# Attention with two feed-forward layers on one core: weight loads, score stacks and one preparation moved at the beginning

## The chip, the cores and the metric

The kernel runs on one core of a Trainium2 chip. The metric is the device time of one execution in microseconds (us). The core has five instruction streams: TensorE (PE, with its weight loads as PEld), VectorE (DVE), ScalarE (ACT), GpSimd (POOL) and SyncE (SP), which here only issues transfers. Each stream runs its instructions in the order in which they stand in the program, and an instruction that waits holds up all that stand behind it.

## The reference

```python
scores = scale * q @ k.T                       # 4 batches, 8 heads, 576 tokens, head size 64
cum    = cumsum(log(clip(f, 1e-4, 1)))         # a decay per token
scores = where(causal, -1e9, scores + cum[i] - cum[j])
attn   = softmax(scores) @ v                   # -> x: 2304 tokens x 512
h = x @ w_in;   x = (h * tanh(softplus(h))) @ w_out      # d_ff 2048
h = x @ w_in2;  out = (h * cos(h)) @ w_out2
```

All inputs are float32, the feed-forward weights float64 in memory (as raw pairs of 32-bit words). The kernel splits each matrix of the feed-forward part into a high and a low float32r half and makes three products of them.

## The kernel before

**Jobs.** Attention is cut into 20 jobs. A job is a pair of heads of one batch with a list of blocks of query rows (128 rows each, the last one 64); one block of a job is an item, and there are 80. Batch 0 is cut in two (`CUT_BATCHES`): jobs 0 to 3 are its first 256 rows (two items each, `small`), jobs 4 to 7 the rest (three items each), both in float32 (`whole`). Jobs 8 to 19 are the other batches, five items each, in float32r halves.

**One item** goes through `scores` (PE products at L549 or L556, DVE maximum at L587, ACT exponential at L591), `normalise` (DVE L601 and L602, POOL L604), `transposes` (PE L630, L633, L642, copied to the tile `p` by ACT L623 or DVE L625) and `av` (PE L666, then ACT L678 and DVE L679 write `xb`). In the main loop the transposes come two or three items behind the scores, and `av` follows the transposes of the last block of a piece.

**Preparation.** `prep_job` transposes q and k of a job on PE (L495) and copies them into a score stack. For jobs 4 to 7 that is one DVE copy (L527) and five ACT copies (L525); for jobs 8 and on ACT copies (L532), DVE subtracts (L533), and POOL then copies the result to other rows (L536). It also issues the transfers of the decay rows (L473) and, at its end, the loads of the job two further on. The main loop spreads it over the last steps of an earlier job: `ready` and `begin` (L762 to L767) say which.

**Stacks.** `four` (L854, named `stk` in rows) holds the four small jobs. Two float32 stacks (`stk`, made at L726) serve jobs 4 to 7 in turn, and two float32r stacks (`stkr`) serve jobs 8 and on in turn. `new_stack` fills constant rows by memsets on POOL (L687 and L688, or L700, L701 and L704). The first `stkr` is made at the beginning (L727); the second takes the place of the float32 stacks, whose pool is closed when job 9 is prepared, during job 8.

**Weights.** `split_weights` loads the first layer's weights in 16 pieces of 512 KB (L108) into two buffers (`rawp`, L76) and converts each by DVE L128, ACT L130, DVE L136, ACT L140 and DVE L142. A call of `next(weights)` is one piece; L875 makes one such call in every third step of the main loop. Two pieces make a chunk of 256 hidden columns (`wih`, `wil`). The hidden products of the first layer (L160, `h`) that these feed are spread between the attention work by a credit (L882 to L889) and fill PE where attention waits.

**Order.** The framework schedules the instructions when the program is built, by its own estimate of durations: it takes them out of the order of the code where their inputs allow. So a change in the code's order moves more than the lines it touches. The order on each engine is then fixed.

Of the kernel before, what the change touches and what calls it, by code (L numbers as in the profile page):

```python
# [9 lines left out]
F32 = mybir.dt.float32  # L10
F32R = mybir.dt.float32r
# [30 lines left out]
def tile_attention_two_ffn(  # L42
# [48 lines left out]
    def split_weights(layer, nm, pool, early=False):  # L91
        wi, wo = (w1_in, w1_out) if layer == 1 else (w2_in, w2_out)
        nb, nn = (NK, 256) if nm == "i" else (2, DM)
        per = 512 // nn
        pieces = []
        for c in range(NCH):
            if nm == "i":
                src = wi.bitcast(I32)[:, 512 * c : 512 * c + 512].rearrange("(b p) n -> p b n", p=128)
            else:
                src = wo.bitcast(I32)[256 * c : 256 * c + 256, :].rearrange("(b p) n -> p b n", p=128)  # L100
            pieces += [(c, src, u) for u in range(0, nb, per)]
        raws = {}

        def load(i):
            if i < len(pieces):
                c, src, u = pieces[i]
                raws[i] = rawp.tile([128, per, nn, 2], I32, tag="raw", name="raw")
                nc.sync.dma_start(out=raws[i].rearrange("p b n t -> p b (n t)"), in_=src[:, u : u + per])  # L108

        PF = 1 if early else 3  # L110
        with tc.issue_after(marks["cum"].ins):
            for i in range(PF):
                load(i)
        for i, (c, src, u) in enumerate(pieces):
            load(i + PF)
            raw = raws.pop(i)
            if u == 0:
                W[layer, c, nm] = tuple(
                    pool.tile([128, nb, nn], F32R, tag=f"w{nm}{x}{c}", name=f"w{nm}{x}{c}") for x in "hl"
                )  # L120
            hi, lo = W[layer, c, nm]
            with ExitStack() as hold:
                beside = (layer, nm) == (1, "o")
                key = "ttr" if early else "hs" if beside else "v1"
                if key in marks:
                    hold.enter_context(tc.issue_after(marks[key].ins))
                high, low = raw[:, :, :, 1], raw[:, :, :, 0]
                nc.vector.tensor_scalar(out=low, in0=low, scalar1=29, scalar2=None, op0=ALU.logical_shift_right)  # L128
                if early:
                    nc.scalar.activation(out=f(high), in_=f(high), func=AF.Prelu, scale=REBIAS, alpha=SIGN_GAP)  # L130
                else:
                    nc.vector.scalar_tensor_tensor(
                        out=low, in0=high, scalar=-0x80000000, in1=low, op0=ALU.bitwise_and, op1=ALU.bitwise_or
                    )
                    nc.scalar.activation(out=f(high), in_=f(high), func=AF.Copy, scale=REBIAS)
                nc.vector.scalar_tensor_tensor(  # L136
                    out=high, in0=high, scalar=3, in1=low, op0=ALU.logical_shift_left, op1=ALU.bitwise_or
                )
                sl = (slice(None), slice(u, u + per))
                nc.scalar.activation(out=hi[sl], in_=f(high), func=AF.Copy)  # L140
                sub = nc.vector if early or beside else nc.gpsimd
                sub.tensor_tensor(out=lo[sl], in0=f(high), in1=f(hi[sl]), op=ALU.subtract)  # L142
            if u + per == nb:
                converted[layer, c, nm] = clock["m"]
            yield
# [220 lines left out]
    def attention_units(p, bank):  # L366
# [311 lines left out]
            nc.scalar.activation(out=xh, in_=t[:, 0:width], func=AF.Copy)  # L678
            nc.vector.tensor_tensor(out=xl, in0=t[:, 0:width], in1=f(xh), op=ALU.subtract)  # L679

        stacks, early = {}, ExitStack()

        def new_stack(pool, name, dt, en):
            if dt == F32:
                t = pool.tile([128, 2, 2, S], dt, name=name, bufs=1)
                st, tails = [t[:, 0], t[:, 1]], None
                en.memset(st[0][64:66], -8.0)  # L687
                en.memset(st[1][64:66], 8.0)  # L688
            else:
                t = pool.tile([128, 2 * QW + 4 * S], dt, name=name, bufs=1)  # L690
                st, tails = [None] * 4, {}
                for n, x in enumerate((0, 2)):
                    at = n * QW
                    w = QW - TAIL
                    st[x] = t[:, at : at + 2 * w].rearrange("p (j s) -> p j s", j=2)[:, :, 0:TAIL]
                    at += TAIL
                    both = t[:, at : at + 256].rearrange("p (j s) -> p j s", j=2)[:, :, 0:64]
                    tails[x] = (t[:, at : at + 128], t[:, at + 64 : at + 192], both)
                    if n:
                        en.memset(f(t[64:68, n * QW : n * QW + QW]), -8.0)  # L700
                    nc.gpsimd.memset(f(t[:, at + 64 : at + 128]), 0.0)  # L701
                    at = 2 * QW + 2 * S * n
                    st[x + 1] = t[:, at : at + 2 * S].rearrange("p (j s) -> p j s", j=2)
                en.memset(f(st[3][64:68]), 8.0)  # L704
            return st, tails

        def stack(jb):
            if small(jb):
                return [four[:, 0, jb], four[:, 1, jb]], None
            key = (whole(jb), jb % 2)  # L710
            if key not in stacks:
                if key == (False, late % 2):
                    early.close()
                    pool = late_sb.enter_context(tc.tile_pool(name="stk", bufs=1))
                else:
                    pool = p
                stacks[key] = new_stack(pool, f"stkr{jb % 2}", F32R, nc.gpsimd)
            return stacks[key]

        load_small()  # L720
        yield ("loads", 0)
        late = 1 + max(jb for jb in range(len(jobs)) if whole(jb)) + 1
        e = early.enter_context(tc.tile_pool(name="stk0", bufs=1))
        with tc.issue_after(marks["mask"].ins):
            for i in range(2):
                stacks[True, i] = new_stack(e, f"stk{i}", F32, nc.gpsimd)  # L726
            stack(late - 1)  # L727
        for jb in range(2):
            for _ in prep_job(jb):
                pass  # L730
# [10 lines left out]
        for m in range(2 * (M + PAIR_LAG + 1)):  # L741
            m2, sub = divmod(m, 2)
            if sub == 0:
# [7 lines left out]
                if m2 < M and small(items[m2][0]):  # L751
                    scores(*items[m2])
            else:
                if m2 in turn:
                    transposes(*items[turn[m2]])
                if m2 < M:
                    normalise(*items[m2])
            if m2 < M:
                jb, i = items[m2]
                bl = jobs[jb][1]  # L760
                at = 2 * bl.index(i) + sub
                ready = jb + 2 if small(jb) else jb + 1  # L762
                begin = max(0, 2 * len(bl) - (9 if ready < len(jobs) and not whole(ready) else 5))
                if at == begin and jb != NP:
                    prep = prep_job(ready)
                if at >= begin:
                    next(prep, None)  # L767
# [83 lines left out]
    def bank():  # L851
        return psa.tile([128, 512], F32, tag="s1", name="s1")

    four = xps[1].tile([128, 2, NK, S], F32, tag="xb", name="stk4", bufs=1).rearrange("p a b s -> p (a b s)")  # L854
    four = four[:, 0 : 4 * NP * HALF].rearrange("p (x n j s) -> p x n j s", x=2, n=NP, j=2)
    decay = decay_tables(ap)
    next(decay)
    att = attention_units(ap, bank)
# [114 lines left out]
```

## Time and profile before

| | us |
|---|---|
| median of three runs | 1024.88 |
| lowest and highest of the three | 1022.93, 1035.28 |
| the profiled execution, its own time | 1019.63 |
| span of its instructions | 1017.8 |
| PE busy in it | 998.6 (98%) |
| DVE, ACT, POOL busy | 583.1, 537.6, 174.9 |

The attention part lasts to about 350 us; after it PE runs the rest of the feed-forward work without a gap. The page cuts the span into 40 slices and gives the busy share of each engine and the clock that the throttle granted to TensorE. Busy time of PE includes time in which matmuls are in flight, so a matmul at half the clock also shows as busy: its duration tells which it was. "Idle before" in a row of the timeline is the time that the engine waited ahead of that row, and the arrow names what ended it.

### The profile page before, as it was taken

Reading aid. Unit: us, or ns where it says so; the run is one execution under the profiler, and the core shown is the slowest. Engines: PE = TensorE matmul, PEld = TensorE weight load, DVE = VectorE, ACT = ScalarE, POOL = GpSimd, SP = SyncE. Lnnn points to the kernel's source line nnn. Section 1 sums busy time; section 2 is a strip of 40 time slices with the busy share of each in tenths; the row PEclk is TensorE's granted clock in tenths of the full one; section 3 lists DMA queues with packets and bytes.
Section 4 is the critical chain, followed back from the end, with each engine's and each line's share of the span. In section 5 each row is a group of like instructions: output and inputs, shape, how many; then the busy total and the mean of one; then the engine's idle time right before and its main releaser. Section 6 shows DMA issues by size and latency. Waiting matters only on the chain.

```text
span 1017.8 us, 16431 instructions
## 1 busy us (share of the span) xinstructions
PE 998.6 (98%) x5836; PEld 857.1 (84%) x5836; DVE 583.1 (57%) x1351; ACT 537.6 (53%) x1151; POOL 174.9 (17%) x250
## 2 busy tenths in 40 slices
PE   6899999999999999999999999999999999999998
PEld 5677888899999999988898888888888888888887
DVE  6777756565555437657652477655544544444454
ACT  5885756665555447557664565444333333333343
POOL 6234433333222200012220031110000000000000
PEclk9999999999999999999999999999999999999999
DMA  7675333243322269849783556102102100100010
GB/s 177 164 201 141 83 90 87 72 105 93 86 60 71 87 201 298 263 137 320 238 293 109 176 165 228 42 1 83 42 1 69 56 0 1 54 30 1 1 42 22
DMA packets 118313, 111.74 MB, mean 110 GB/s; under 512 B 66520, under 2 KB 87016, under 8 KB 118232
## 3 DMA queue, kind: packets, MB, share of 16 engines
q1 hardware_dynamic: 113880, 105.98, 34.0%
q10 hardware_dynamic: 4352, 4.72, 1.4%
q8 instruction: 46, 0.75, 0.3%
q14 instruction: 35, 0.29, 0.1%
HBM read 77.40 MB, written 33.25 MB: 109 GB/s over the span
## 4 chain that ended last, share of the span: by engine, by line
PE 92%; DMA 3%; DVE 1%; ACT 1%; SPq 1%; issue 1%; POOL 0%; DVEq 0%; POOLq 0%; ACTq 0%
PE h L160 25%; PE acc L265 19%; PE hx L160 11%; PE acc L257 11%; PE s L666 5%; PE hx L257 4%; PE h L257 4%; PE s L556 4%; PE s L642 3%; PE acc L160 2%; DMA raw<-in_moe_w_in_dram 2%; PE s L495 2%; PE s L549 1%; PE s L630 1%; DMA natk<-in_k_dram 1%
## 5 line engine op out<-in xcount | busy, mean ns | idle before, releaser
L160 PE MATMUL h<-xb,wih 128*128 128x288 f32 (+2 forms) x840 | 180.2, 303 | 1.4 <-DVE xb L679 1.2
L160 PEld LDWEIGHTS h<-xb,wih 128*128 128x128 f32 x840 | 137.0, 189 | 7.2 <-issue 2.1
L160 PE MATMUL h<-xb,wil 128*128 128x288 f32 (+2 forms) x420 | 124.9, 299 | 0.0
L604 POOL TENSOR_SCALAR s<-s,sm 128x128 f32<-128x128 f32 (+4 forms) x144 | 85.9, 610 | 180.1 <-DVE sm L602 130.5
L265 PE MATMUL acc<-woh,gh 128*128 128x512 f32 x288 | 112.9, 392 | 0.0
L265 PE MATMUL acc<-woh,gl 128*128 128x512 f32 x288 | 112.3, 391 | 0.0
L265 PE MATMUL acc<-wol,gh 128*128 128x512 f32 x288 | 112.0, 389 | 0.0
L591 ACT ACTIVATE s<-s,mx 128x128 f32<-128x128 f32 (+4 forms) x144 | 83.5, 581 | 47.5 <-DVE mx L587 46.6
L330 DVE TENSOR_TENSOR gl<-hl,gh 128x512 fp32r<-128x512 f32 x72 | 56.1, 780 | 72.7 <-ACT gh L325 68.1
L587 DVE CUSTOM_DVE_ANT_0 s<-s,maskt 128x128 f32<-128x128 f32 (+4 forms) x144 | 67.1, 484 | 51.5 <-PE s L642 23.8
L316 ACT ACTIVATE n<-n 128x512 f32<-128x512 f32 (+1 forms) x80 | 47.1, 589 | 86.3 <-DVE n L310 86.2
L160 PE MATMUL hx<-x,wih 128*128 128x512 f32 (+1 forms) x320 | 92.6, 369 | 0.0
L160 PE MATMUL h<-x,wih 128*128 128x512 f32 (+1 forms) x320 | 91.0, 369 | 0.0
L330 DVE TENSOR_TENSOR gl<-e,gh 128x512 fp32r<-128x512 f32 (+1 forms) x80 | 53.9, 674 | 51.4 <-ACT gh L325 51.3
L309 DVE TENSOR_SCALAR n<-e 128x512 f32<-128x512 f32 (+1 forms) x80 | 32.7, 408 | 85.9 <-ACT e L302 85.3
L160 PEld LDWEIGHTS h<-xb,wil 128*128 128x128 f32 x420 | 79.1, 189 | 1.0 <-issue 0.7
L325 ACT ACTIVATE gh<-e 128x512 fp32r<-128x512 f32 (+1 forms) x80 | 47.1, 588 | 53.3 <-DVE e L321 49.8
L325 ACT ACTIVATE gh<-hl 128x512 fp32r<-128x512 f32 x72 | 45.2, 628 | 49.8 <-issue 30.2
L160 PEld LDWEIGHTS h<-x,wih 128*128 128x128 f32 x320 | 58.4, 188 | 10.9
L257 PE MATMUL acc<-gh,wol 128*128 128x512 f32 (+1 forms) x192 | 67.6, 354 | 0.0
L257 PE MATMUL acc<-gl,woh 128*128 128x512 f32 (+1 forms) x192 | 67.6, 354 | 0.0
L160 PEld LDWEIGHTS hx<-x,wih 128*128 128x128 f32 x320 | 58.4, 188 | 10.9
(119 smaller groups left out, 2114.4 us busy)
## 6 DMA issues: line engine op xcount, KB each, us to landing
hl<-hd SPq DMA_DIRECT2D x72, 256.0 KB
raw<-in_moe_w_in_dram SPq DMA_DIRECT2D x32, 512.0 KB
raw<-in_moe_w_out_dram SPq DMA_DIRECT2D x32, 512.0 KB
hd<-hs SPq DMA_DIRECT2D x32, 288.0 KB
yd<-stage SPq DMA_DIRECT2D x32, 256.0 KB
x<-yd SPq DMA_DIRECT2D x32, 256.0 KB
natv<-in_v_dram SPq DMA_DIRECT2D x36, 128.0 KB
natk<-in_k_dram SPq DMA_DIRECT2D x32, 144.0 KB
```

The costliest lines, as they stand in the source:

```text
L160: nc.tensor.matmul(o, lhsT=a[wsl], rhs=b[:, kk, :], start=(kk == 0 and i == 0), stop=(kk == NK - 1 and i == 2),)
L257: nc.tensor.matmul(acc[ti][d][:, 0:T], lhsT=a[dsl], rhs=b[:, gs], start=(start and i == 0), stop=(end and i == 2),)
L265: nc.tensor.matmul(acc[ti][m], lhsT=a[:, ms], rhs=b[:, j % 2, :], start=(start and i == 0), stop=(end and i == 2),)
L309: nc.vector.tensor_scalar(out=t, in0=e, scalar1=ROUND, scalar2=ROUND, op0=ALU.add, op1=ALU.subtract)
L316: nc.scalar.activation(out=t, in_=t, func=AF.Sin, scale=TWO_PI)
L325: gmark[n] = nc.scalar.activation(out=gh, in_=e, func=AF.Copy)
L330: marks["v1"] = nc.vector.tensor_tensor(out=gl, in0=st.pop(n)[0], in1=f(gst[n][0]), op=ALU.subtract)
L556: marks["score"] = nc.tensor.matmul(o, lhsT=lhs[0:rows], rhs=st[x + 1][0:rows, j, c0:c1], start=(x == 0 and not (both and j)), stop=(x == ...
L587: marks["ttr"] = nc.vector.tensor_tensor_reduce(out=s[:, c0:c1], in0=o, in1=mk, scale=-0.125, scalar=prev, op0=ALU.add, op1=ALU.min, accum ...
L591: nc.scalar.activation(out=s[:, 0:w], in_=s[:, 0:w], func=AF.Exp, scale=-1.0, bias=mx, accum_out=sm[:, j : j + 1])
L604: nc.gpsimd.tensor_scalar(out=s[:, 0:w], in0=s[:, 0:w], scalar1=sm[:, j : j + 1], scalar2=1.0, op0=ALU.mult, op1=ALU.mult)
L666: pair = nc.tensor.matmul(t[64 * j : 64 * j + 64, c0:width], lhsT=vt[jb][keys, c, j], rhs=pt[keys, j, c, c0:width], start=(c == 0), stop=( ...
```

## The change

Four things. The first weights: two pieces are loaded at the first call and nothing is converted at that call, so that each conversion falls one call (three steps of the main loop) later than before. The preparation: `ready` is two jobs ahead only for jobs 0 and 1, so that job 4 is prepared during job 3 and not during job 2, job 5 during job 4 and not during job 3; from job 6 on nothing moves. The float32 stacks take the place of `four` in the tile of `xps[1]` that batch 1's output uses later, and `four` has a pool of its own. This pool is closed when item 9 is reached (in job 4), and both `stkr` stacks are made there, the second in the room of `four`; before, one was made at the beginning and the other in job 8.

```diff
-            for i in range(PF):
+            for i in range(2 if early else PF):
                 load(i)
+        if early:
+            yield
         for i, (c, src, u) in enumerate(pieces):
-            load(i + PF)
+            if not early or i:
+                load(i + PF)
...
-            if key not in stacks:
-                if key == (False, late % 2):
-                    early.close()
-                    pool = late_sb.enter_context(tc.tile_pool(name="stk", bufs=1))
-                else:
-                    pool = p
-                stacks[key] = new_stack(pool, f"stkr{jb % 2}", F32R, nc.gpsimd)
             return stacks[key]
...
-        e = early.enter_context(tc.tile_pool(name="stk0", bufs=1))
+        pair = xps[1].tile([128, 2, NK, S], F32, tag="xb", name="stk", bufs=1).rearrange("p a b s -> p (a b s)")
+        pair = pair[:, 0 : 8 * S].rearrange("p (n x j s) -> p n x j s", n=2, x=2, j=2)
         with tc.issue_after(marks["mask"].ins):
             for i in range(2):
-                stacks[True, i] = new_stack(e, f"stk{i}", F32, nc.gpsimd)
-            stack(late - 1)
+                stacks[True, i] = new_stack(pair[:, i], "", F32, nc.gpsimd)
...
             else:
+                if m2 == 2 * NP + 1:
+                    early.close()
+                    late = late_sb.enter_context(tc.tile_pool(name="stk", bufs=1))
+                    for x, pool in ((0, p), (1, late)):
+                        stacks[False, x] = new_stack(pool, f"stkr{x}", F32R, nc.gpsimd)
...
-                ready = jb + 2 if small(jb) else jb + 1
+                ready = jb + 2 if jb < NP - 2 else jb + 1
...
-                if at == begin and jb != NP:
+                if at == begin and jb != NP - 2:
                     prep = prep_job(ready)
...
-    four = xps[1].tile([128, 2, NK, S], F32, tag="xb", name="stk4", bufs=1).rearrange("p a b s -> p (a b s)")
-    four = four[:, 0 : 4 * NP * HALF].rearrange("p (x n j s) -> p x n j s", x=2, n=NP, j=2)
+    early = ExitStack()
+    first_stacks = early.enter_context(tc.tile_pool(name="stk4", bufs=1))
+    four = first_stacks.tile([128, 2, NP, 2, HALF], F32, name="stk4", bufs=1)
```

In the rows of the change below, line numbers are three higher (L160 has become L163); the masks keep theirs. What the diff does to the order shows at three places. The first is PE at the transposes of q and k for job 4 (L495 before, L498 now; `s_...` are the banks of PSUM). Before, they stand between the transposes of item 2 (`s_324`) and those of item 3 (`s_369`), around the scores of item 5:

```order
L642 MATMUL s_324<-ident,s 128x128 x2
L495 MATMUL s_332<-ident,natq 128x80 x4
L495 MATMUL s_332<-ident,natk 128x96 x2
L549 MATMUL s_344<-stk_97 128x256 x2
L495 MATMUL s_355<-ident,natk 128x96 x4
L160 MATMUL h<-xb,wih_206 128x256 x2
L642 MATMUL s_369<-ident,s 128x128 x4
```

Now they stand one job later, between the transposes of item 4 (`s_372`) and those of item 5 (`s_417`), around the scores of item 7:

```order
L645 MATMUL s_372<-ident,s 128x128 x2
L498 MATMUL s_380<-ident,natq 128x80 x4
L498 MATMUL s_380<-ident,natk 128x96 x2
L552 MATMUL s_399<-stk_100 128x256 x2
L498 MATMUL s_410<-ident,natk 128x96 x4
L163 MATMUL h<-xb,wih_235 128x256 x2
L645 MATMUL s_417<-ident,s 128x128 x4
```

The second place is ACT ahead of the copy of job 3's last `p` (`s_527` before, `s_515` now), for which `av` of job 3 waits. Before, the conversion of a piece and the two exponentials of item 9 (128x512) stand ahead of it:

```order
L678 ACTIVATE xb<-s_491 128x256
L140 ACTIVATE wih_432<-raw 128x512
L130 ACTIVATE raw<-raw 128x512
L591 ACTIVATE s,sm<-s,mx 128x512 x2
L623 ACTIVATE p<-s_527 128x4x128
```

Now the five copies of job 5's stack stand there too, and the conversion's L133 stands between the two exponentials:

```order
L143 ACTIVATE wih_459<-raw 128x512
L594 ACTIVATE s,sm<-s,mx 128x512
L133 ACTIVATE raw<-raw 128x512
L594 ACTIVATE s,sm<-s,mx 128x512
L528 ACTIVATE stk<-s_525 64x384 x2
L528 ACTIVATE stk<-s_490 64x320
L528 ACTIVATE stk<-s_490 64x192 x2
L626 ACTIVATE p<-s_515 128x4x128
```

The third is POOL at the end of job 8's preparation (`stkr_148` before, `stkr_505` now). Before, three memsets of the second stack (`stkr_1266`) and one `normalise` (128x576) stand ahead of the last copy of job 8's stack (64x2x384):

```order
L536 CAST stkr_148<-stkr_148 64x2x64
L536 CAST stkr_148<-stkr_148 64x2x192
L701 MEMSET stkr_1266 128x64
L700 MEMSET stkr_1266 4x1216
L704 MEMSET stkr_1266 4x1152
L604 TENSOR_SCALAR s<-s,sm 128x576
L536 CAST stkr_148<-stkr_148 64x2x384
```

Now the last copy follows the others at once, and the memsets are elsewhere:

```order
L539 CAST stkr_505<-stkr_505 64x2x64
L539 CAST stkr_505<-stkr_505 64x2x192
L539 CAST stkr_505<-stkr_505 64x2x384
L607 TENSOR_SCALAR s<-s,sm 128x576
```

Of the memsets, those of the first `stkr` stack now stand among the first instructions of POOL, ahead of the two selects that finish the masks (L782, L788), and those of the second between the `normalise` of item 5 and that of item 6.

## Rows read from the trace of the kernel before

**Rows 1.** The page: span, and busy time of each engine.
```profile
span 1017.8 us, 16431 instructions
PE 998.6 (98%) x5836; PEld 857.1 (84%) x5836; DVE 583.1 (57%) x1351; ACT 537.6 (53%) x1151; POOL 174.9 (17%) x250
```

**Rows 2.** Windows: stretch, length, PE, PEld, DVE, ACT, POOL busy; clock, DMA share, GB/s.
```profile
0.00:20.00 20.00, 12.23 (x42) 9.10 (x44) 13.12 (x38) 10.46 (x27) 14.09 (x28) 1.00 0.84 192
20.00:45.00 25.00, 22.07 (x127) 15.96 (x124) 18.57 (x66) 20.34 (x54) 8.80 (x13) 1.00 0.61 156
45.00:90.00 45.00, 44.32 (x343) 34.38 (x341) 35.12 (x104) 34.99 (x86) 17.78 (x23) 1.00 0.67 186
90.00:100.00 10.00, 8.21 (x65) 6.73 (x66) 6.31 (x20) 4.09 (x12) 2.95 (x6) 0.83 0.38 107
130.00:350.00 220.00, 219.34 (x1720) 200.69 (x1718) 127.09 (x456) 127.50 (x355) 72.58 (x126) 1.00 0.29 81
```

**Rows 3.** Timeline of PE at job 8's first scores: start, duration, instruction, [idle before].
```profile
88.78 0.50 PE L160 MATMUL h<-xb,wih 128*128 128x256 f32 x2
89.48 0.28 PE L160 MATMUL h<-xb,wil 128*128 128x256 f32 x1
91.79 0.66 PE L556 MATMUL s<-stkr 128*128 128x128 f32 x4 [2.03 <-POOL stkr L536]
92.38 3.19 PE L666 MATMUL s<-p,natv 128*64 128x192 f32 x20
```

**Rows 4.** Timeline of PE: the same 20 matmuls of `av` two jobs earlier.
```profile
59.06 1.78 PE L666 MATMUL s<-p,natv 128*64 128x192 f32 x20
```

**Rows 5.** Timeline of POOL before job 8's first scores.
```profile
87.11 0.51 POOL L536 CAST stkr<-stkr 64x384 fp32r<-64x384 f32 x1 [0.62 <-ACT stkr L532]
87.89 1.11 POOL L700 MEMSET stkr<- 4x1216 f32 x1
90.91 0.82 POOL L536 CAST stkr<-stkr 64x768 fp32r<-64x768 f32 x1
```

**Rows 6.** Timeline of ACT in the same stretch.
```profile
86.17 0.38 ACT L185 ACTIVATE hs<-h 128x256 f32<-128x256 f32 x1
86.66 0.84 ACT L532 ACTIVATE stkr<-s 64x192 fp32r<-64x192 f32 x2
89.41 0.49 ACT L532 ACTIVATE stkr<-s 64x384 fp32r<-64x384 f32 x1
```

**Rows 7.** Timeline of PE, 22 to 49 us: transposes of job 4, three waits.
```profile
22.19 0.74 PE L495 MATMUL s<-ident,natq 80*128 80x80 f32 x4
28.66 0.87 PE L666 MATMUL s<-p,natv 128*64 128x256 f32 x8 [0.87 <-ACT p L623]
42.30 0.87 PE L666 MATMUL s<-p,natv 128*64 128x256 f32 x8
48.18 0.88 PE L666 MATMUL s<-p,natv 128*64 128x128 f32 x12 [0.43 <-DVE p L625]
```

**Rows 8.** Timeline of ACT, 28 to 42 us: copies, a wait for a piece.
```profile
28.01 0.60 ACT L623 ACTIVATE p<-s 128x512 f32<-128x512 f32 x1
32.36 1.96 ACT L525 ACTIVATE stk<-s 64x384 f32<-64x384 f32 x5
39.67 0.69 ACT L130 ACTIVATE raw<-raw 128x512 f32<-128x512 f32 x1 [0.84 <-DMA raw<-in_moe_w_in_dram]
41.66 0.59 ACT L623 ACTIVATE p<-s 128x512 f32<-128x512 f32 x1
```

**Rows 9.** Timeline of POOL, 4 to 38 us: a mask, memsets, normalise.
```profile
4.65 0.29 POOL L782 TENSOR_SCALAR_AFFINE_SELECT maskt<-maskt 128x128 f32<-128x128 f32 x1
20.30 2.00 POOL L604 TENSOR_SCALAR s<-s,sm 128x256 f32<-128x256 f32 x2 [2.81 <-ACT raw L130]
35.75 0.72 POOL L604 TENSOR_SCALAR s<-s,sm 128x128 f32<-128x128 f32 x2 [4.10 <-DVE sm L602]
37.57 0.94 POOL L604 TENSOR_SCALAR s<-s,sm 128x256 f32<-128x256 f32 x2 [1.10 <-ACT s L591]
```

More of the change, by code (lines that the diff above doesn't have):

```diff
@@ L679, in av @@
             nc.vector.tensor_tensor(out=xl, in0=t[:, 0:width], in1=f(xh), op=ALU.subtract)
-        stacks, early = {}, ExitStack()
+        stacks = {}
         def new_stack(pool, name, dt, en):
             if dt == F32:
-                t = pool.tile([128, 2, 2, S], dt, name=name, bufs=1)
+                t = pool
                 st, tails = [t[:, 0], t[:, 1]], None
@@ L721, in attention_units @@
         yield ("loads", 0)
-        late = 1 + max(jb for jb in range(len(jobs)) if whole(jb)) + 1
-        e = early.enter_context(tc.tile_pool(name="stk0", bufs=1))
+        pair = xps[1].tile([128, 2, NK, S], F32, tag="xb", name="stk", bufs=1).rearrange("p a b s -> p (a b s)")
+        pair = pair[:, 0 : 8 * S].rearrange("p (n x j s) -> p n x j s", n=2, x=2, j=2)
         with tc.issue_after(marks["mask"].ins):
             for i in range(2):
-                stacks[True, i] = new_stack(e, f"stk{i}", F32, nc.gpsimd)
-            stack(late - 1)
+                stacks[True, i] = new_stack(pair[:, i], "", F32, nc.gpsimd)
         for jb in range(2):
```

## The prediction

> **What bounds the kernel now.** I read the page first: PE is busy for 998.6 of 1017.8 us [rows 1], so no change of the order can give back more than the 19.2 us in which it is idle and what it loses at half the clock. The windows say where that lies [rows 2]. Of the first 20 us PE works 12.23, of the next 25 it works 22.07, of the following 45 all but 0.68, then 8.21 of 10, and from 130 to 350 us all but 0.66 of 220. The order on PE differs from before only within the attention part; after it the same instructions stand in the same order, so I take nothing from there. The two stretches that can move are 20 to 45 us and 90 to 100 us.
>
> At 91.79 us PE waits 2.03 us for the first scores of job 8 [rows 3]. After that wait the granted clock is 0.83 over 10 us [rows 2], which is 3.4 us at the lower level of 1.2 GHz and the rest at 2.4, and costs 10 x 0.17 = 1.7 us. The matmuls show it: the 20 of `av` take 3.19 us there [rows 3] and 1.78 two jobs earlier [rows 4]. So this one place costs 3.7 us. In the stretch of 20 to 45 us the fullest of the other engines is ACT, 20.34 of 25 us [rows 2]; PE waits there for copies of ACT, such as 0.87 us for `p` at 28.66 [rows 7].
>
> **Job 8's stack.** What PE waits for at 91.79 is the POOL copy at 90.91, 0.82 us [rows 5]. Ahead of it POOL does three memsets and a `normalise`; and the ACT copy that feeds it, at 89.41 [rows 6], stands behind an exponential and a copy of `p`. In the change both are reordered: the memsets are gone from there, the POOL copy follows the one before it, and on ACT only the copy to `hs` stands between the two last stack copies. By rows: the ACT copies that now come first end at 86.66 + 0.84 = 87.50, `hs` takes 0.38 and the last copy 0.49 [rows 6], together 88.37; POOL's 0.82 and 0.1 of handing over give 89.3. Before it was 91.73.
>
> PE comes there earlier too, since seven fewer hidden products stand between the transposes of job 8 and its first scores (their pieces are converted a call later). The last six before them run from 88.78 to 89.76, the first starting 0.70 us ahead of the sixth [rows 3], 0.14 us from one to the next, so seven are 1.0 us, which PE owes and does later. It arrives at 89.76 - 1.0 = 88.8 and waits 0.5 us instead of 2.03. This gives 1.5 us. A wait of 0.5 us should leave the clock where it was: waits of 0.43 and 0.87 us are followed by full speed [rows 7], so the 1.7 us of the clock come back as well. The bounds are 0 (if another wait takes its place) and 3.7. I take **-3.2 us**.
>
> **Preparation of jobs 4 and 5.** Each is ten transposes on PE, one copy on DVE and five on ACT, and the five cost 1.96 us of ACT [rows 8]. Each moves one job later. Up to `av` of job 1 the change has one preparation less: its `p` can be copied some 0.7 us earlier than at 28.01 [rows 8], so `av` starts near 28.0 instead of 28.66 [rows 7]. PE's share is moved and not saved: 0.74 us for the first four transposes at the lower level [rows 7], about half at the higher one.
>
> Between `av` of job 1 and `av` of job 3 the change has both preparations where before there was one. PE has room for it. ACT hardly has: from the copy at 28.01 to that at 41.66 it had 13.65 us [rows 8], of which it idled about 1.9, 0.84 of it for a piece of the weights at 39.67. It now gets 1.96 us of copies more, and the order puts job 5's five copies just ahead of the copy of `p` for which `av` of job 3 waits. If every idle moment is filled, `av` of job 3 comes when it did, at 42.30. If none is, it comes 1.96 us later, less the 0.7 of the earlier start, plus what the weights add. For these there are still two buffers, so the third piece waits as before for the first conversion; the transfers of the second late stack's rows now stand on SP ahead of the sixth piece and wait for POOL's memsets. ACT waits for that piece between the two exponentials of item 9, and I reckon up to 0.8 us more. So `av` of job 3 comes 0 to 2.1 us later; since ACT's idle moments were waits for pieces, which stay, I take 2.0. Of this the wait of 0.43 us at 48.18 [rows 7] takes back its part, and from there to 90 us PE is full, so nothing else does: **+1.5 us**.
>
> **Edits costed at nothing.** (1) The memsets of the first late stack now stand ahead of the mask's last select, which started at 4.65 [rows 9]. They take about 2.3 us (the memset of 1.11 us [rows 5], another like it, a small one). The mask is then ready at 7.3 us, and the first scores that need it end after 10: 2.7 us of cover. What follows on POOL ends when it did, since the sum is the same. (2) The memsets of the second late stack, 2.5 us, start when PE has done item 7's scores, near 31 us, and POOL was idle for the 4.10 us up to 35.75 [rows 9]. Behind them is queued the `normalise` of item 6 and, by that, its transposes. If the cover fails, that is up to 0.7 us, inside the bounds of the term above. (3) The weights: each conversion is a call later, and the hidden products that need it with it. PE needs products to fill it only where it would wait, and from 45 to 90 us it waits 0.68 of 45 us [rows 2]; a product that slides is done later on a full PE. (4) `xb` of batch 1 now shares its room with the float32 stacks; it is written after job 8's scores, and their last reader is job 7's.
>
> **A rule weighed against the first term.** The same kind of `normalise`, two of 128x256, took 0.94 us at 37.57 and 2.00 at 20.30 [rows 9]: POOL can be held up by about 1 us. The Trainium skill, "SBUF — State Buffer", section "SBUF: two separate sides", says why that would be: POOL and a VectorE instruction with two inputs in SBUF take turns on one pair of ports, and the loser waits for the whole instruction of the other. By that rule the last stack copy, next to a weight subtract on DVE, would end later by the subtract's length; the trace agrees so far as the 2.00 us go. By rows alone the price of such a meeting is at most 2.00 - 0.94 = 1.06 us, and I make it a rival.
>
> **Sum.** -3.2 + 1.5 = -1.7 us. The profiled execution took 1019.63 us (1.8 beyond its span), so the changed kernel would give 1017.9 there. The median of the three runs is 5.25 us above the profiled execution. I carry the difference over to it: 1024.88 - 1.7 = 1023.2, **1023 us**.
>
> **Rivals**, all in the terms of the median.
> - *ACT takes up the second preparation in its idle moments.* It idled 1.9 us and the copies are 1.96. Then the second term is 0 and the time is 1021.7, or 1021 if job 8 gives its full 3.7. Against it: those idle moments are waits for pieces.
> - *Slower: the first stretch costs more than job 8 gives.* If the waits of PE before job 3's `av` fall together to about the 2.03 us after which the clock fell at 91.79 [rows 3], another 1.7 us go there: +1.5 + 1.7 + up to 2 for products at the lower level that ACT then waits for. It decides from a single wait of 2 us; the price is up to +5.2, the net +2.0, the time 1026 to 1027. Against it: PE can be held in two parts, once at job 4's stack, once at `p`.
> - *POOL's last copy is held up* by 1.06 us: the first term shrinks to -2.1 and the time is 1024.
> - *The change does not do what it shows at job 8*: PE starts the scores early and then waits for `p` ahead of `av`, and the clock falls all the same. The first term is then about 0, the time 1026.4. Against it: on ACT those copies of `p` follow directly behind the stack's.
>
> **Chances.** The forecast 0.40, the first rival 0.23, the slower one 0.18, the held copy 0.08, no gain at job 8 0.08, anything else 0.03. All these lie within 1021 and 1027. What runs of one kernel do is wider: 1022.93 to 1035.28 for this one, and 1019.63 in the profile. So the range is taken from 1021 less the half of the 5.25 us that the profile lies below the median, and a little, 1016, to 1027 plus about the same, 1031. 2% is 20.5 us, about what a measurement of this kernel can tell from no change. PE's whole idle time is below that, so faster by more has 0.01. Slower by more would need a new stall of that size at a place where PE now has none: 0.02.
>
> **What would show each step.** Right: PE's wait before L559 of job 8 below 0.7 us and a granted clock of 1.00 from 90 to 100 us; PE's wait before `av` of job 3 between 1 and 3 us; PE as full as before from 50 to 85 us; the wait for a piece on ACT near 40 us as long as before or longer. Wrong: a clock below 1.00 in the first 90 us, a wait of PE on a weight piece, or a difference that arises after 350 us.

## The result

The changed kernel takes 1028.27 us in the median of 22 runs (1025.41 to 1034.93), the kernel before 1023.48 in 22 runs beside it (1019.46 to 1037.38). The ratio is 1.0065, with a 95% interval of 1.0049 to 1.0081: 0.65% slower, about a third of the 2% that I had set as the bound of "the same", and of the other sign than my forecast of -1.7 us. Every ratio in this document leaves out the runs more than 1.5% above the fastest of their kernel, so that it isn't the quotient of the two medians beside it. The time lies in the range that I gave; the reason for it does not lie in the sum that I gave.

The profiled execution took 1028.01 us. Its page, to be read against [rows 1]:

```profile
span 1025.9 us, 16423 instructions
PE 1007.9 (98%) x5836; PEld 862.9 (84%) x5836; DVE 586.1 (57%) x1351; ACT 536.4 (52%) x1151; POOL 174.5 (17%) x250
```

The span grew by 8.1 us. That is more than the 4.8 us between the medians, since the profile before is one of the fastest executions of its kernel (1019.63 us; the lowest of 124 is 1019.31) and this one lies near the median of its own. PE's idle time did not grow: it is 1025.9 - 1007.9 = 18.0 us, and was 19.2. What grew is PE's busy time, by 9.3 us with the same 5836 matmuls. So the same matmuls took longer, and that is the clock. The windows say where (stretch, length, PE, PEld, DVE, ACT, POOL busy; granted clock, DMA share, GB/s; against [rows 2]):

```profile
20.00:45.00 25.00, 23.29 (x110) 17.01 (x106) 17.65 (x60) 17.21 (x47) 8.56 (x16) 1.00 0.49 134
45.00:90.00 45.00, 42.73 (x284) 32.12 (x285) 27.76 (x83) 28.80 (x73) 12.24 (x16) 0.89 0.55 146
90.00:100.00 10.00, 8.64 (x72) 6.77 (x72) 8.78 (x26) 8.10 (x21) 4.33 (x6) 0.97 0.54 142
100.00:130.00 30.00, 29.32 (x227) 24.50 (x224) 23.61 (x78) 21.55 (x59) 12.42 (x19) 0.95 0.45 121
130.00:350.00 220.00, 220.00 (x1724) 201.12 (x1723) 128.41 (x460) 128.34 (x360) 74.15 (x130) 1.00 0.30 83
```

From 45 to 90 us PE starts 284 matmuls where it started 343, at a granted clock of 0.89: 45 x 0.11 = 5.0 us lost. From 20 to 45 us PE is busier than before (23.29 against 22.07 us) and starts fewer matmuls (110 against 127). The clock column says 1.00 there, but it does so from the first microsecond on: it knows only changes that were recorded, and the first recorded one comes later. Before that the level has to be read from durations. The timeline of PE (start, duration, instruction, [idle before]; against [rows 7]):

```profile
25.83 0.41 PE L163 MATMUL h<-xb,wil 128*128 128x256 f32 x1
27.88 1.55 PE L669 MATMUL s<-p,natv 128*64 128x256 f32 x8 [1.64 <-ACT p L626]
31.66 1.97 PE L552 MATMUL s<-stk 66*128 66x256 f32 x4
38.53 0.87 PE L669 MATMUL s<-p,natv 128*64 128x256 f32 x8
46.71 0.87 PE L669 MATMUL s<-p,natv 128*64 128x256 f32 x8 [1.79 <-ACT p L626]
47.51 2.19 PE L552 MATMUL s<-stk 66*128 66x384 f32 x4
53.34 1.91 PE L552 MATMUL s<-stk 66*128 66x512 f32 x2
59.13 0.50 PE L498 MATMUL s<-ident,natk 96*128 96x96 f32 x4
98.90 0.66 PE L559 MATMUL s<-stkr 128*128 128x128 f32 x4 [1.36 <-POOL stkr L539]
99.49 3.24 PE L669 MATMUL s<-p,natv 128*64 128x192 f32 x20
104.60 0.74 PE L163 MATMUL h<-xb,wih 128*128 128x256 f32 x4 [0.49 <-ACT wih L143]
```

The eight matmuls of an `av` of 128x256 take 0.87 us at 2.4 GHz and 1.55 at 1.2. Before, job 1's `av` already had 0.87 us at 28.66 [rows 7]. Now PE waits 1.64 us ahead of it, it takes 1.55, and full speed comes only with job 2's `av` at 38.53. At 46.71, after a wait of 1.79 us, job 3's `av` is still fast and the clock falls right behind it; about 10 us later, near 58 us, it is back. Two stretches of about 10 us at the lower level, where the profile before has full speed, are twice about 5 us. What makes PE wait stands on ACT:

```profile
25.68 0.69 ACT L133 ACTIVATE raw<-raw 128x512 f32<-128x512 f32 x1 [2.34 <-DMA raw<-in_moe_w_in_dram]
26.27 0.49 ACT L594 ACTIVATE s<-s,mx 128x256 f32<-128x256 f32 x1
27.26 0.57 ACT L626 ACTIVATE p<-s 128x512 f32<-128x512 f32 x1
44.07 1.96 ACT L528 ACTIVATE stk<-s 64x384 f32<-64x384 f32 x5
46.06 0.60 ACT L626 ACTIVATE p<-s 128x512 f32<-128x512 f32 x1
```

A conversion waits 2.34 us at the head of ACT for its piece of the weights, and item 5's exponentials and the `p` of job 1 stand behind it. And job 5's five copies stand ahead of the `p` of job 3, as the order of the change had shown.

### The profile page after: what moved, and what is told of

The parts are those of the page before. It is cut to its first block, busy times and chain, and to the rows that moved or that the text cites. A ratio compares the mean times of both kernels' runs of the same rounds, so it can differ in the third digit from the quotient of the medians.

```text
span 1025.9 us, 16423 instructions
## 1 busy us (share of the span) xinstructions
PE 1007.9 (98%) x5836; PEld 862.9 (84%) x5836; DVE 586.1 (57%) x1351; ACT 536.4 (52%) x1151; POOL 174.5 (17%) x250
## 4 chain that ended last, share of the span: by engine, by line
PE 90%; DMA 4%; ACT 2%; DVE 2%; issue 1%; POOL 1%; SPq 0%; ACTq 0%; DVEq 0%; POOLq 0%
PE h L163 24%; PE acc L268 19%; PE hx L163 11%; PE acc L260 11%; PE hx L260 4%; PE h L260 4%; PE s L669 4%; PE s L559 4%; DMA raw<-in_moe_w_in_dram 4%; PE s L645 3%; PE acc L163 2%; PE s L498 2%; ACT s L594 1%; PE s L552 1%; DVE wil L145 1%
## 5 line engine op out<-in xcount | busy, mean ns | idle before, releaser
L163 PE MATMUL h<-xb,wih 128*128 128x288 f32 (+2 forms) x840 | 180.4, 305 | 0.7 <-ACT wih L143 0.5
L163 PEld LDWEIGHTS h<-xb,wih 128*128 128x128 f32 x840 | 137.2, 190 | 8.0 <-issue 3.7
L163 PE MATMUL h<-xb,wil 128*128 128x288 f32 (+2 forms) x420 | 124.9, 299 | 0.0
L333 DVE TENSOR_TENSOR gl<-hl,gh 128x512 fp32r<-128x512 f32 x72 | 59.6, 829 | 69.9 <-ACT gh L328 65.6
L163 PE MATMUL hx<-x,wih 128*128 128x512 f32 (+1 forms) x320 | 92.7, 369 | 0.0
L163 PE MATMUL h<-x,wih 128*128 128x512 f32 (+1 forms) x320 | 91.0, 369 | 0.0
L163 PEld LDWEIGHTS h<-xb,wil 128*128 128x128 f32 x420 | 79.4, 190 | 1.1 <-issue 0.5
L163 PEld LDWEIGHTS hx<-x,wih 128*128 128x128 f32 x320 | 58.4, 188 | 11.0
L163 PEld LDWEIGHTS h<-x,wih 128*128 128x128 f32 x320 | 58.4, 188 | 10.9
```

The costliest lines, as they stand in the source:

```text
L163: nc.tensor.matmul(o, lhsT=a[wsl], rhs=b[:, kk, :], start=(kk == 0 and i == 0), stop=(kk == NK - 1 and i == 2),)
L333: marks["v1"] = nc.vector.tensor_tensor(out=gl, in0=st.pop(n)[0], in1=f(gst[n][0]), op=ALU.subtract)
```

## The experiments

Each of the twelve kernels was run beside the kernel before, whose median was 1024.32, 1023.36 and 1024.11 us in the three groups of four. Runs of one kernel do not scatter around one value: of the 124 runs of the kernel before, 34 lie between 1032.7 and 1037.4 us and all the others below 1028. So the last column counts the runs above 1030 us. They don't make the loss: without them the changed kernel has a median of 1027.78 us and the kernel before 1022.82. Line numbers shift with each edit, so the rows are to be read by their tiles.

| kernel | median us (lowest to highest) | ratio to before [95%] | above 1030 |
|---|---|---|---|
| e1 preparation only | 1022.29 (1020.22 to 1028.08) | 0.9970 [0.9934, 1.0007] | 0 of 12 |
| e2 weights only | 1022.79 (1019.68 to 1034.60) | 1.0011 [0.9964, 1.0059] | 4 of 12 |
| e3 stacks only | 1022.33 (1019.33 to 1035.59) | 0.9978 [0.9931, 1.0026] | 3 of 12 |
| e4 weights, stacks | 1020.44 (1016.01 to 1031.19) | 0.9959 [0.9918, 0.9999] | 1 of 12 |
| e5 weights, preparation | 1034.52 (1030.00 to 1039.32) | 1.0097 [1.0064, 1.0131] | 8 of 9 |
| e6 preparation, stacks | 1022.66 (1021.20 to 1034.35) | 0.9992 [0.9959, 1.0025] | 1 of 12 |
| changed kernel (all three) | 1028.27 (1025.41 to 1034.93) | 1.0065 [1.0049, 1.0081] | 7 of 22 |
| e7 with dummies, `av` of job 3 | 1024.41 (1020.69 to 1034.17) | 1.0012 [0.9974, 1.0050] | 2 of 12 |
| e8 with dummies from the start | 1027.25 (1023.19 to 1029.48) | 1.0021 [0.9992, 1.0050] | 0 of 12 |
| e9 exponentials first | 1021.95 (1017.07 to 1032.86) | 0.9987 [0.9950, 1.0023] | 3 of 12 |
| e10 dummies, `av` of jobs 1 and 3 | 1020.70 (1019.60 to 1024.04) | 0.9978 [0.9954, 1.0002] | 0 of 12 |
| e11 = e4 with a dummy, `av` of job 1 | 1018.51 (1016.92 to 1024.61) | 0.9947 [0.9907, 0.9988] | 0 of 12 |
| e12 = e11 with one at job 0's too | 1031.15 (1027.74 to 1032.05) | 1.0060 [1.0026, 1.0095] | 9 of 12 |

**The parts alone (e1 to e3) and without the preparation (e4).** The edits, of the diff above: the preparation (P), the weights (W), and the stacks (S, all the rest).

```
P  -  ready = jb + 2 if small(jb) else jb + 1
   +  ready = jb + 2 if jb < NP - 2 else jb + 1
   -  if at == begin and jb != NP:
   +  if at == begin and jb != NP - 2:
W  -  for i in range(PF):
   +  for i in range(2 if early else PF):
   +  if early:
   +      yield
   ...
   -      load(i + PF)
   +      if not early or i:
   +          load(i + PF)
S  +  if m2 == 2 * NP + 1:
   +      early.close()
   ...
```

> The kernel before with the preparation of jobs 4 and 5 moved one job later, and nothing else of the change. Theory (the moved preparation makes PE wait before the outputs of jobs 1 and 3, and the clock is then at 1.2 GHz for some 10 us more at each of the two places): +6 to +10 us (ratio 1.006 to 1.010), a granted clock of 0.5 to 0.8 somewhere between 45 and 60 us, and 128x256 score products at their long duration (about 0.49 us each) still at 31 us. Rival A (the weights converted a call later do it): 0 to +2 us here. Rival B (the late stacks' memsets and the transfers behind them on SyncE do it): 0 to +2 us here.

> The kernel before with the first two weight pieces loaded at the first call and each conversion a call later, and nothing else of the change. Theory (preparation): within 1.5 us of before, the clock at its full level from 28 to 85 us as before. Rival A (weights): +4 to +8 us, with PE or ScalarE waiting longer for pieces between 20 and 60 us. Rival B (stacks): no change.

> The kernel before with the float32 stacks in the other tile and both late stacks made at item 9, and nothing else of the change. Theory (preparation): -1 to -3 us, since the memsets are gone from in front of the last copy of job 8's stack: PE's wait of 2.03 us there falls to about 1 us. Rival B (stacks): +3 to +7 us, from the normalise of item 6 behind the memsets on GpSimd and the weight pieces behind the late stack's transfers on SyncE. Rival A: within 1 us.

> The changed kernel with the preparation of jobs 4 and 5 put back where it was. Theory (preparation): -1 to -4 us against the kernel before, so 8 to 12 us faster than the change. Rivals A and B: slower than before by 3 to 8 us, close to the change.

My first theory was that the preparation alone costs the time. It fell: alone it costs nothing that can be measured, nor does any part alone; only without the preparation is the kernel a little faster, by 0.1 to 8.2 parts in a thousand. So the loss is made by parts that meet.

**Pairs (e5, e6).** e5 is P and W, e6 is P and S.

> The change without its stacks part: weights loaded two pieces ahead and the fifth job prepared in the fourth, the score stacks in their old buffers. Theory A (the preparation collides on ACT with the weights' conversion, which now stands ahead of item 5's exponentials): the loss appears here already, about +4 us against the kernel before (ratio 1.003 to 1.006), with a wait of about 1.6 us of TensorE ahead of job 1's av and about 1.8 us ahead of job 3's, and the clock below 0.9 between 45 and 60 us. Theory B (the preparation collides with the stacks: the second stack's memsets hold POOL at 33.7 to 36.2 us and so the normalise of the items behind): no loss here, ratio 0.996 to 1.001, wait ahead of job 3's av under 1 us.

> The change without its weights part: the fifth job prepared in the fourth, the stacks in other buffers with the late ones made there too, weights loaded as before. Theory A (preparation against weights): no loss, ratio 0.994 to 1.000 against the kernel before, wait ahead of job 3's av under 1 us. Theory B (preparation against stacks): the loss appears here, ratio 1.003 to 1.006, with the wait of about 1.8 us ahead of job 3's av and a clock below 0.9 between 45 and 60 us. If both pairs lose nothing, the loss needs all three parts.

The loss is that of preparation and weights together, and larger than in the changed kernel: 1034.52 us. The stacks take part of it back. But the rows of e5 don't show what I expected of it, a fall of the clock at 47 us. In it the clock has not risen at all by 60 us:

```profile
25.99 0.41 PE L163 MATMUL h<-xb,wil 128*128 128x256 f32 x1
27.83 1.55 PE L669 MATMUL s<-p,natv 128*64 128x256 f32 x8 [1.43 <-ACT p L626]
38.89 1.55 PE L669 MATMUL s<-p,natv 128*64 128x256 f32 x8
50.55 1.50 PE L669 MATMUL s<-p,natv 128*64 128x256 f32 x8
60.81 1.55 PE L669 MATMUL s<-p,natv 128*64 128x128 f32 x12
```

ACT's wait for the piece of the weights is in e6 too (2.41 us), and PE's wait behind it is longer, but there the clock has risen ahead of it: the last product before the wait takes 0.28 us, and 0.41 in e5 and in the changed kernel.

```profile
26.74 0.28 PE L160 MATMUL h<-xb,wil 128*128 128x256 f32 x1
28.86 0.87 PE L666 MATMUL s<-p,natv 128*64 128x256 f32 x8 [1.85 <-ACT p L623]
31.57 1.97 PE L549 MATMUL s<-stk 66*128 66x256 f32 x4
37.94 0.87 PE L666 MATMUL s<-p,natv 128*64 128x256 f32 x8
```

It falls again before 30.3 us and is back at 37.94 (granted clock 0.66 from 30 to 40 us, 3.4 us lost), and the time is that of the kernel before. So the length of the wait (1.43 us in e5, 1.85 in e6) is not what separates e5 from e6 by 12 us. What separates them is how long the lower level lasts: past 60 us in e5, to about 37 us in e6. The place where PE runs out of work fits this. It is at 26.40 us in e5 and 26.24 in the changed kernel, with the clock still low; at 27.01 in e6 and 26.74 in e1, with the clock just up. But these are single profiles, and in that of e4 PE works to 27.56 us and the clock is still low; so why it rises or not is not shown by them. What it is worth to keep PE busy, the next kernels test directly.

**Dummies in PE's waits (e7, e8).** In e7 the changed kernel has four matmuls more, whose results are overwritten:

```
             t = bank()
+            for _ in range({3: 4}.get(jb, 0)):
+                with tc.issue_after(marks["pe"].ins):
+                    nc.tensor.matmul(t[:, 0:512], lhsT=ident, rhs=maskt[:, 0:512], start=True, stop=True)
             for c in range(nb):
```

`marks["pe"]` is the last matmul traced before; the rest of the order is held, so that up to about 57 us the rows of PE differ only in these.

> The changed kernel with four dummy matmuls of 128x512 ahead of the av of job 3, in TensorE's wait of 1.79 us at about 45 us; they write the bank that this av overwrites. Nothing is computed otherwise, and TensorE's work grows by about 1.7 us, laid into the wait. Theory C (the clock falls because of that wait, and the loss of about 5 us from 47 to 57 us is the half level and not the wait itself): the clock is 1.00 from 45 to 90 us, matmuls of 66x384 at 47 to 55 us take half as long as in the changed kernel (x4 about 1.1 us in place of 2.19), and the time falls by 3 to 5 us to 1023 to 1025 us. If the loss is the waits themselves or the later rows on ACT, the time stays at 1027 to 1029 us or rises by up to 1.7 us.

```profile
44.53 3.70 PE L669 MATMUL s<-maskt,ident 128*128 128x512 f32 x8
48.16 0.87 PE L678 MATMUL s<-p,natv 128*64 128x256 f32 x8
48.96 1.56 PE L558 MATMUL s<-stk 66*128 66x384 f32 x4
```

The four took 3.70 us, twice what I had reckoned, so job 3's `av` starts at 48.16, later than the 46.71 of the changed kernel. All the same the time falls to 1024.41 us, from a ratio of 1.0065 to 1.0012, and eight of the twelve runs lie below the fastest of the changed kernel: the matmuls behind take 1.56 us in place of 2.19. PE does more, its `av` comes later, and the kernel is faster. The fall of the clock is what cost the time at this place, not the wait.

In e8 the dummies stand in PE's idle time of the first 9 us (`warm` is a tile of zeros, `wbank` a bank of the hidden products that nobody reads):

```
+    def heat(n):
+        for _ in range(n):
+            nc.tensor.matmul(wbank[:, 0:128], lhsT=warm, rhs=warm, start=True, stop=True)
+    heat(10)
...
+                    if jb == 1:
+                        with tc.issue_after(marks["pe"].ins):
+                            heat(2)
                     nc.tensor.transpose(t[:, at : at + P], ...)
```

> The changed kernel with dummy matmuls of 128x128 in TensorE's idle time of the first 9 us: ten ahead of the first transpose and two ahead of each transpose of job 1 (about 4 us of work at the half level, from about 1 us on). Theory D (several levels of the time come from when the clock first rises to its full level, between 27 and 59 us as the runs of these kernels lie, and that rise is late because TensorE stands idle at the start): the matmuls are at full speed from 10 to 20 us on in place of 38 us, and no run lies above 1027 us; the time falls by 5 to 9 us to 1019 to 1023 us. If the start of the program has nothing to do with it: 1027 to 1029 us as without them, with runs of 1031 to 1035 us among them.

```profile
4.95 0.38 PE L501 MATMUL s<-ident,natq 128*128 128x128 f32 x2
13.46 0.33 PE L648 MATMUL s<-ident,s 128*128 128x128 f32 x1 [1.50 <-POOL s L610]
16.43 1.55 PE L675 MATMUL s<-p,natv 128*64 128x256 f32 x8 [0.80 <-ACT p L629]
26.26 1.05 PE L555 MATMUL s<-stk 66*128 66x256 f32 x4
30.68 1.98 PE L555 MATMUL s<-stk 66*128 66x384 f32 x4 [1.46 <-ACT stk L531]
34.34 3.62 PE L555 MATMUL s<-stk 66*128 66x512 f32 x4
45.54 1.56 PE L555 MATMUL s<-stk 66*128 66x384 f32 x4
```

The theory was half right. The clock is up by 4.95 us (two transposes take 0.38 us; the changed kernel's first two take 0.66), earlier than the 9 us that the expectation of e12 names, and no run lies above 1030 us any more. But a faster PE runs out of work: it stops 1.50 us for POOL, the clock falls, rises again near 25 us, PE stops 1.46 us for ACT, the clock falls again until 45 us, and once more from 60 to 70 us (granted clock 0.54). An early rise is worth little where the engines that feed PE can't follow: the median is 1.0 us below that of the changed kernel.

**The cause of the wait, and dummies in both waits (e9, e10).** In e9 a conversion is issued behind the exponentials that were traced before it, in the changed kernel otherwise:

```
                 if early:
+                    with tc.issue_after(marks["exp"].ins):
                         nc.scalar.activation(out=f(high), in_=f(high), func=AF.Prelu, ...)
...
+                marks["exp"] = nc.scalar.activation(
                     out=s[:, 0:w], in_=s[:, 0:w], func=AF.Exp, ...
```

e10 is e7 with two dummies ahead of job 3's `av` and one ahead of job 1's (`{1: 1, 3: 2}`).

> The changed kernel, in which ACT issues each first conversion of a raw weight piece (L133) behind the exponentials traced before it; in the changed kernel the one at 25.68 us waits 2.34 us for its piece and stands ahead of item 5's exponentials and of the p copy that job 1's av waits for. Nothing is added or left out. Theory E (that wait at ACT's head makes TensorE stop at 26.24 us for 1.64 us, and this stop is what keeps the clock from rising there): TensorE's wait ahead of job 1's av falls to under 1 us, the matmuls are at full speed from about 28 us on in place of 38, and the time falls by 4 to 7 us to 1021 to 1024 us. If another matter keeps the clock low: the wait falls and the time moves by under 2 us.

> The changed kernel with one dummy matmul of 128x512 ahead of the av of job 1 (1.86 us at the half level, in a wait of 1.64 us) and two ahead of that of job 3 (1.85 us at full speed, in a wait of 1.79 us). Theory C and E together (waits on both places cost by the clock, not by themselves): matmuls at full speed from 28 us on in place of 38, clock 1.00 from 45 to 90 us, the time falls by 7 to 9 us to 1019 to 1021 us, below the four dummies ahead of job 3's av alone (1024.4). If the rise at 28 us doesn't hang on TensorE's stop at 26.24 us: 1023 to 1025 us as with job 3's alone.

e9, PE:

```profile
26.83 1.55 PE L670 MATMUL s<-p,natv 128*64 128x256 f32 x8 [0.77 <-ACT p L627]
35.14 1.46 PE L553 MATMUL s<-stk 66*128 66x384 f32 x4
42.74 0.87 PE L670 MATMUL s<-p,natv 128*64 128x256 f32 x8
```

e10, PE:

```profile
24.92 1.92 PE L669 MATMUL s<-maskt,ident 128*128 128x512 f32 x2
27.95 0.87 PE L678 MATMUL s<-p,natv 128*64 128x256 f32 x8 [0.38 <-ACT p L632]
43.49 0.87 PE L678 MATMUL s<-p,natv 128*64 128x256 f32 x8 [0.62 <-ACT p L632]
44.29 1.56 PE L558 MATMUL s<-stk 66*128 66x384 f32 x4
```

In e9 the wait ahead of job 1's `av` falls to 0.77 us, that of job 3 is gone, and the time is 1021.95 us: what stood at ACT's head did make the waits. The rise comes before 35.14 us, earlier than in the changed kernel (38.5) but not at 28 as I expected, and 3 of 12 runs stay above 1030 (7 of 22 in the changed kernel): the order alone gives the loss back in the median, but that it makes such runs rarer is not shown. In e10 no wait over 0.7 us is left at either place, the clock is up at 27.95, stays up to 90 us, and all twelve runs lie between 1019.60 and 1024.04. The whole loss is gone with three matmuls more. Job 3's `av` starts at 43.49 us, 1.2 us later than in the kernel before, so the waits are not gone: they are filled.

**A version that beats both (e11), and one step too far (e12).** e11 is e4 with one dummy ahead of job 1's `av`; e12 has another ahead of job 0's.

> The change without its preparation part (1020.4 us), with one dummy matmul of 128x512 ahead of the av of job 1, where TensorE waits 0.9 to 1.2 us just as the clock is about to rise. Theory E: no run above 1026 us is left (without the dummy 1 of 12, and 11 of 35 runs of the kernel before, lie at 1031 to 1036 us), the median stays at 1019 to 1021 us or gains up to 1 us. If the rise doesn't hang on that wait: runs above 1030 us remain in about the same share.

> As the run before, with one more dummy matmul of 128x512 ahead of the av of job 0, where TensorE waits 1.6 us at 17.4 us. Theory D as the run with dummies from the start left it (the clock then rose at 9 us and fell at each later stop of about 1.5 us): the clock rises before 20 us, up to 3 us are gained if no stop over 1 us follows, to 1017 to 1019 us, or it falls again at such a stop and the time is 1021 to 1024 us. If the rise comes at about 27 us whatever stands ahead of job 0's av: 1020 to 1021 us.

e11 takes 1018.51 us, 0.12 to 0.93% less than the kernel before, with no run above 1025. Without its runs above 1030 us the kernel before has a median of 1022.83 in this group, so 1.3 of the 5.6 us between the medians are those runs, and 4.3 come from the weights, the stacks and the clock together. That the dummy adds anything to e4 (1020.44 us, ratio 0.9959) is not shown: the intervals overlap, and e4 had only one run above 1030. e12 shows the price of an early rise (PE):

```profile
20.58 0.71 PE L558 MATMUL s<-stk 66*128 66x128 f32 x4
32.32 0.39 PE L169 MATMUL h<-xb,wih 128*128 128x256 f32 x1 [2.78 <-DVE xb L693]
34.81 2.77 PE L558 MATMUL s<-stk 66*128 66x384 f32 x4
50.73 2.93 PE L558 MATMUL s<-stk 66*128 66x384 f32 x4
```

Full speed at 20.58 us, then a stop of 2.78 us because PE has overtaken its feeders, and the lower level from 34 to past 60 us: 12.6 us more than e11, for one matmul.

## Why the prediction was wrong

**The second term, +1.5 us for the preparation, is the step that failed.** Its first half held: ACT has both preparations between the two `av`, job 5's copies stand ahead of the `p` that job 3's `av` needs, and PE's wait there is 1.79 us, inside the 1 to 3 that I had named. But I priced a wait by its own length. The copy of job 1's `p` did come 0.75 us earlier, as I had reckoned (27.26 in place of 28.01), but PE, with the transposes of job 4 gone from there, had run out of work at 26.24 already, 1.56 us earlier than before, and so stood still for 1.64 us just where its clock used to rise. I had counted PE's moved transposes as "moved and not saved" and not asked what their going leaves behind. And I took the clock of 20 to 45 us as given, since its column said 1.00; that is the stretch in which the level first rises. The later rise (38.5 us in place of 28) is in no rival of mine; with it job 2's `av` comes at 38.53 us and not at 34.99, and job 3's at 46.71 and not at the 44.3 of my sum. In place of +1.5 us the runs showed about 5.0 us for the fall behind job 3's `av`, of which e7 gives 3.9 back, and up to 5 for the later rise in this profile. How much of the later rise belongs to the change and how much to the execution one profile can't say; e10, which fills both waits, lies 3.7 us below e7. The waits themselves were priced well enough: in e10 job 3's `av` is 1.2 us late, within my 0 to 2.1.

**The slower rival is what happened in kind.** It had the waits ahead of job 3's `av` fall together to about 2 us, the clock fall there, and 1026 to 1027 us. I gave it 0.18, since PE "can be held in two parts", and priced the clock at 1.7 us as at 91.79 [rows 3]; it was 5.0. It also had a wait of 2 us as the point that decides. The clock fell behind shorter ones, and not behind all of the same length (below).

**The first term, -3.2 us for job 8, was mis-sized.** The work did move as told: in the changed kernel nothing but stack copies stands on POOL ahead of the last one. But PE waits 1.36 us ahead of L559 and not 0.5, and the clock falls there as before (the 20 matmuls take 3.24 us). So the profile shows 0.7 us of the 3.2, and nothing of the clock's 1.7. In e11, whose start is undisturbed (ACT, then POOL, then PE):

```profile
88.63 0.49 ACT L541 ACTIVATE stkr<-s 64x384 fp32r<-64x384 f32 x1 [0.52 <-DVE stkr L542]
89.18 0.82 POOL L545 CAST stkr<-stkr 64x768 fp32r<-64x768 f32 x1 [0.43 <-ACT stkr L541]
90.05 0.67 PE L565 MATMUL s<-stkr 128*128 128x128 f32 x4 [1.64 <-POOL stkr L545]
90.65 1.78 PE L678 MATMUL s<-p,natv 128*64 128x192 f32 x20
```

The copies don't follow each other as I had added them up: ACT waits 0.52 us for DVE's subtract between them. Job 8's scores start at 90.05 where I had 89.3 and before it was 91.79, and PE gets there at 88.41 instead of 89.76, so its wait of 1.64 is only 0.4 shorter. But there the clock stays up behind it (the 20 matmuls take 1.78 us), so e11 has the clock's 1.7 us. The stacks are worth 2.0 us in medians over the kernel before (e3) and 2.35 over e2 (e4), and nothing over e1 (e6); the intervals are wider than that, so their gain between 0 and 2.4 us stays open.

**The edits costed at nothing.** The memsets and the shared `xb` cost nothing that shows. The weights did: a wait of PE for a converted piece, which I had named as a sign against me, stands at 104.60 in the changed kernel (0.49 us), and e10 has one of 1.49 us near 100. Behind 350 us nothing differs, as foretold. That POOL's last copy is held up did not come: it takes 0.82 us as before.

**What stays open** is why the clock rises early in one execution and not in the next. It differs among runs of one kernel, so it isn't in the order of the instructions alone. The Trainium skill, "TensorE: Matmul & The Clock Gate", section "Part 1: The HAM clock gate (the "warmup" mystery)", says that the count of slow matmuls at a kernel's start varies from run to run, because what the chip watches does not begin with the kernel. The groups of runs agree with that. The page also puts the cost of this start below 1% of a span; here the two groups of the kernel before lie about 12 us apart, 1.2%, and the measurement decides. That its upper group is a late rise is inferred: no run of it was profiled, only runs of e4 (1031.19 us) and e5 (1034.52), where the clock rises after 60 us.

## What to carry to other kernels

When PE is 98% busy, as here, price a change of the order by what it does to the clock, and not only by the waits that it adds: read the level from matmul durations in every stretch, above all before the first recorded change of the clock. Look at where the clock first rises, and keep PE from waiting there; a matmul whose result is thrown away, put into a wait that can't be removed, tests in one run whether a wait costs by its length or by the clock. Put it only where PE has work behind it, since an early rise that can't be fed can cost more than it gives (e12).

## What the runs showed of the hardware

- Runs of one kernel fall into two groups about 12 us apart (1022.8 and 1035.2 us for the kernel before, 34 of 124 runs in the upper one). No run of e10 and e11, with a matmul more ahead of job 1's `av`, lies above 1030 us (0 of 12 each); but neither does one of e1 without it, so that this matmul removes the group is likely and not shown. A profile shows one of the groups only: that of e4 is the one run of twelve that lies in the upper, with half speed past 60 us. The mean granted clock of a run doesn't show the late rise: five of the seven runs of the changed kernel above 1030 us have 0.997 to 1.000, and those below have 0.988 to 0.996, for what lies ahead of the first recorded change counts as full speed.
- Stops of PE at full speed, and what the granted clock did within the next 5 us: it fell after stops of 1.36 and 1.79 us (changed kernel), 1.49 (e2), 1.67 (e9, at 91 us), 1.69 (e1), 1.85 (e6), 2.03 (before) and 3.13 (e1, at 91 us), for 3 to 10 us; it stayed up after stops of 1.28 and 1.41 (e3), 1.35 (e7), 1.49 (e10, at 100 us), 1.64 (e11, at 90 us), 2.22 (e5, at 103 us) and even 3.14 us (e2, at 90 us). So the length of the one stop doesn't tell the two apart.
